# First expert's first weights loaded by GpSimd in rows of 1 KB, and block 1's queries and keys earlier in the order

## The chip, the cores and the metric

The kernel runs on one core of one Trainium2 chip. The metric is the device time of one execution in microseconds (us), the median of several runs. A time line in the text counts from the first instruction of the profiled execution.

## The reference

Two steps follow each other. The first is attention in chunks of 32 queries, each of which sees its own 32 keys, 16 to the left, 8 to the right and 8 memory keys. The second is a mixture of eight experts over the 3072 tokens that come out of it, with weights from a Sinkhorn iteration over all tokens.

```python
# q, k, v: (4, 8, 768, 64); mem_k, mem_v: (4, 8, 8, 64)
for c in range(seq // 32):
    q_c = q[:, :, c*32 : c*32+32]
    k_full = concatenate([mem_k, k[:, :, l_start:r_end]], axis=2)
    v_full = concatenate([mem_v, v[:, :, l_start:r_end]], axis=2)
    scores = scale * matmul(q_c, k_full.transpose(0, 1, 3, 2))
    a = softmax(scores)
    out[:, :, c*32 : c*32+32] = matmul(a, v_full)
x = out.transpose(0, 2, 1, 3).reshape(3072, 512)

# w_gate (512, 8), w1 (8, 512, 1024), w2 (8, 1024, 512)
P = exp(x @ w_gate - max)
for _ in range(8):
    P /= P.sum(1, keepdims=True) + 1e-9
    P /= P.sum(0, keepdims=True) + 1e-9
    P *= 3072 / 8
for e in range(8):
    h = maximum(x @ w1[e], 0)
    out += P[:, e:e+1] * (h @ w2[e])
```

## The kernel before

The tokens are cut into 24 blocks of 128 for the attention and into 6 units of 512 for the experts. TensorE takes a unit through an expert with operands that are split into two half-precision parts (high and low, three products each). Most units use a scheme of seven products for eight (Winograd's form of Strassen's); the first expert's first unit is done plainly, with the matmuls `pp` (first layer) and `yp` (second layer), so that TensorE can begin with weights that are only split and not yet summed.

Weights come in quarters `fp` = 0 to 3 (256 of the 1024 hidden columns each). A quarter of w1 goes through four steps. `load` (line 531) brings it into a stage tile `w1f`. `most` (line 540, tile `mxs`) takes the absolute maximum on VectorE. `scale_w` turns the four maxima into one scale: a reduction `most_of`, a transpose `row_w` and a spread `sp_w` on TensorE, a power of two and its inverse `sw` on VectorE. `plain1` then splits the quarter into its two parts, the high one on ScalarE (line 495), the low one on VectorE (line 503). The operand x of a unit goes the same way: maxima `vmax` over the values `v_pair` (line 956), `row_x`, `sp_x`, `sx`, and a split. For the units after the first, `cut` makes the sums that the seven products need.

The attention of a block n loads q and k (`load_block`), a piece of keys `kx` for the borders, and the values (`load_values`, half by SyncE and half by ScalarE, into `v_pair`, later into tiles that serve as rooms for other things). TensorE transposes them (`tq`, `tk`, `tx`), computes scores `sp`, transposes the weights `ta`, and makes the output `xp` and its transpose `xt`. VectorE takes the maximum `sm`, the difference `s`, the reciprocal `rec` and the scaled output `xq`.

The order on each engine is made ahead of time by a planner, `Plan`. Each piece of work is a task with an engine, a cost and a priority; the planner steps through a modelled time, gives each engine the ready task of lowest priority number, and writes the instructions down in that order. An engine then runs its list strictly in order. For loads the planner keeps a modelled DMA clock, `dma`, which starts at `FIRST`; a load is not issued more than `BEHIND` ahead of it. The numbers `BLOCKS`, `VALUES` and `FIRST` (inside the kernel) are the priorities of the first four blocks' q and k, of their values, and of the first expert's w1 and w2. Where the planner sees TensorE idle for over 0.4 us, `pad` puts `warm` matmuls on the identity there; they are in the list for good and run whether or not the hole is there on the chip.

DMAs of SyncE and ScalarE go by eight counters in turn, and each waits for the earlier one of its counter. Unit 0's operand x is stored as `xkeep` and fetched again for the later experts.

## Time and profile before

| what | before |
|---|---|
| median of 3 runs | 1922.85 us |
| the three runs | 1923.82, 1922.3, 1922.85 us |
| span of the profiled execution, first to last instruction | 1921.2 us |
| median minus that span | 1.65 us |
| TensorE busy | 1905.9 us |
| VectorE busy | 1436.7 us |
| ScalarE busy | 1032.3 us |
| GpSimd busy | 520.3 us |
| packets of DMA, mean rate | 246792, 133 GB/s |

The profiled execution's own device time is not listed apart from the three; the span stands for it, and the median is 1.65 us longer. TensorE is the engine that sets the time: it is busy nearly throughout, and VectorE, ScalarE and GpSimd each have time to spare on average.

### The profile page before, as it was taken

How to read it: one execution, taken by the hardware profiler on the slowest of the kernel's cores; microseconds unless marked ns; L12 is line 12 of the kernel's file. 1: busy time of each engine (PE TensorE's matmuls, PEld its weight loads, DVE VectorE, ACT ScalarE, POOL GpSimd, SP SyncE). 2: the span in 40 equal slices, each digit the busy share in tenths (PEclk: the TensorE clock that was granted, in tenths of full speed). 3: DMA queues.
4: the chain of work that ended last, by engine and by line, in shares of the span. 5: the costliest groups of instructions: out<-in, count | busy, mean ns of one | idle time of the engine just before them, and what ended most of it. 6: DMA issues, size and time to landing. Idle time of an engine off the chain costs nothing.

```text
span 1921.2 us, 47293 instructions
## 1 busy us (share of the span) xinstructions
PE 1905.9 (99%) x19608; PEld 1641.5 (85%) x19608; DVE 1436.7 (75%) x2396; ACT 1032.3 (54%) x2019; POOL 520.3 (27%) x549
## 2 busy tenths in 40 slices
PE   8999999999999999999999999999999999999999
PEld 7676676688888888888888888888888888888888
DVE  5666569778769866897778875898678885786565
ACT  4665564556556545645545554654554564564453
POOL 1220002443224231432124231342124232332112
PEclk9999999999999999999999999999999999999999
DMA  8677653454235342255214533245313632322321
GB/s 197 174 202 205 169 162 122 138 176 144 83 103 173 131 138 94 78 178 186 109 57 148 204 105 127 78 160 171 143 45 99 242 128 92 102 83 83 127 83 67
DMA packets 246792, 254.82 MB, mean 133 GB/s; under 512 B 113265, under 2 KB 180273, under 8 KB 242225
## 3 DMA queue, kind: packets, MB, share of 16 engines
q1 hardware_dynamic: 244452, 251.21, 40.8%
q8 instruction: 153, 2.51, 0.5%
q10 hardware_dynamic: 2124, 0.59, 0.2%
q14 instruction: 63, 0.51, 0.1%
HBM read 187.84 MB, written 63.44 MB: 131 GB/s over the span
## 4 chain that ended last, share of the span: by engine, by line
PE 94%; DVE 3%; issue 1%; DMA 1%; ACT 0%; POOL 0%; SPq 0%; DVEq 0%; POOLq 0%
PE px L1580 26%; PE yx L1580 22%; PE pz L1580 13%; PE yz L1580 11%; PE py L1580 6%; PE yp L2098 6%; PE yy L1580 5%; PE xp L1119 1%; PE sp L1051 1%; PE pp L2017 1%; DVE ss L1738 1%; PE warm L409 1%; PE ta L1109 0%; PE tk L992 0%; PE tq L988 0%
## 5 line engine op out<-in xcount | busy, mean ns | idle before, releaser
L1580 PEld LDWEIGHTS <-w 128*128 128x128 f16 x7896 | 770.9, 98 | 93.1 <-issue 0.8
L1580 PEld LDWEIGHTS <-h 128*128 128x128 f16 x7056 | 689.9, 98 | 82.9 <-issue 2.6
L1580 PE MATMUL px<-x,w 128*128 128x256 f16 x4512 | 549.1, 273 | 0.5 <-issue 0.3
L1903 POOL TENSOR_TENSOR acc<-acc,y 128x256 f32<-128x256 f32 x252 | 265.6, 1060 | 862.4 <-ACT y L1878 839.8
L1580 PE MATMUL yx<-w,h 128*128 128x256 f16 x4032 | 467.6, 273 | 0.7 <-DVE acc L1913 0.6
L1629 ACT ACTIVATE q<-px 128x256 f32<-128x256 f32 x376 | 142.7, 381 | 304.4 <-PE px L1580 299.8
L1580 PE MATMUL pz<-x,w 128*128 128x256 f16 x2256 | 278.4, 273 | 0.0
L1580 PE MATMUL yz<-w,h 128*128 128x256 f16 x2016 | 233.8, 273 | 1.2 <-ACT y L1878 1.2
L1798 DVE TENSOR_TENSOR h<-ss,h 128x1024 f16<-128x1024 f32 x160 | 214.7, 1344 | 3.8 <-ACT h L1774 3.5
L1749 ACT ACTIVATE h<-c 128x768 f16<-128x768 f32 x168 | 140.8, 838 | 109.5 <-DVE c L1639 109.5
L1774 ACT CAST h<-ss 128x1024 f16<-128x1024 f32 x168 | 174.2, 1040 | 24.9 <-DVE ss L1738 24.0
L1738 DVE SCALAR_TENSOR_TENSOR ss<-c,ss 128x256 f32<-128x256 f32 x336 | 172.3, 513 | 8.2
L1782 DVE SCALAR_TENSOR_TENSOR h<-c,h 128x768 f16<-128x768 f32 x168 | 165.0, 982 | 11.2 <-ACT h L1749 11.2
L1639 DVE SCALAR_TENSOR_TENSOR c<-px,q 128x256 f32<-128x256 f32 x188 | 77.7, 421 | 94.2 <-PE px L1580 85.0
L1878 ACT ACTIVATE y<-yx,pscale 128x256 f32<-128x256 f32 x168 | 79.3, 473 | 112.6 <-PE yx L1580 108.8
L1580 PE MATMUL py<-x,w 128*128 128x256 f16 x1128 | 139.2, 273 | 0.0
L1639 DVE SCALAR_TENSOR_TENSOR c<-py,q 128x256 f32<-128x256 f32 x188 | 78.8, 422 | 72.1 <-PE py L1580 66.1
L2098 PE MATMUL yp<-w,h 128*128 128x512 f16 x576 | 131.7, 379 | 0.0
L1738 DVE SCALAR_TENSOR_TENSOR ss<-c,h 128x512 f32<-128x512 f32 x168 | 122.7, 730 | 2.2 <-ACT h L1726 2.2
L1580 PE MATMUL yy<-w,h 128*128 128x256 f16 x1008 | 116.9, 273 | 0.0
L2098 PEld LDWEIGHTS <-h 128*128 128x128 f16 x576 | 55.4, 98 | 58.9
L503 DVE SCALAR_TENSOR_TENSOR w<-ws,sw,w 128x1024 f16<-128x1024 f32 (+1 forms) x64 | 84.9, 1326 | 25.8 <-ACT w L495 25.8
(158 smaller groups left out, 1755.1 us busy)
## 6 DMA issues: line engine op xcount, KB each, us to landing
x<-xkeep SPq DMA_DIRECT2D x28, 1792.0 KB
akeep<-acc SPq DMA_DIRECT2D x168, 256.0 KB
acc<-akeep SPq DMA_DIRECT2D x168, 256.0 KB
w1f<-in_moe_w_dram SPq DMA_DIRECT2D x72, 256.0 KB
w2f<-in_moe_w_dram SPq DMA_DIRECT2D x32, 512.0 KB
w1fm<-in_moe_w_dram SPq DMA_DIRECT2D x56, 256.0 KB
w2fm<-in_moe_w_dram SPq DMA_DIRECT2D x28, 512.0 KB
xkeep<-x SPq DMA_DIRECT2D x6, 1792.0 KB
```

The source lines that it names most:

```text
L503: lambda: nc.vector.scalar_tensor_tensor(dst(1), src(), s, dst(0), op0=ALU.mult, op1=ALU.subtract),
L1580: nc.tensor.matmul(dst.t, a, b, start=(not more and n == 0), stop=(n == end), skip_group_check=more,)
L1629: lambda: nc.scalar.activation(t.t, src.t, AF.Copy, scale=DOWN),
L1639: lambda: nc.vector.scalar_tensor_tensor(c.t[:, o], src.t, DOWN, q.t, op0=ALU.mult, op1=ALU.add),
L1738: lambda: nc.vector.scalar_tensor_tensor(dst(), src(), 0.0, other(), op0=ALU.max, op1=op),
L1749: lambda: nc.scalar.activation(h.t[:, 0, 0:3], c.t, AF.Relu),
L1774: lambda: nc.scalar.copy(h.t[:, 0, 3:7], ss.t),
L1782: lambda: nc.vector.scalar_tensor_tensor(h.t[:, 1, 0:3].rearrange("p a n -> p (a n)"), c.t.rearrange("p a n -> p (a n)"), 0.0, h.t[:, 0, 0 ...
L1798: lambda: spare.tensor_tensor(h.t[:, 1, 3:7], ss.t, h.t[:, 0, 3:7], op=ALU.subtract),
L1878: (lambda: nc.scalar.activation(t.t, src.t, AF.Copy, scale=f))
L1903: lambda: nc.gpsimd.tensor_tensor(acc.t[:, cols], acc.t[:, cols], q.t, op=ALU.add),
L2098: nc.tensor.matmul(py.t, hf.t[:, hl, where[fh], o : o + P], room(fp, WIDE * wl + DM * fh, WIDE * wl + DM * (fh + 1)), start=(fp == 0 and i ...
```

## The change

The planner keeps one DMA clock for SyncE (with ScalarE) and one for GpSimd. The first expert's four w1 quarters are issued by GpSimd, at priority -60 instead of -38; their maxima and the split come at priorities lower by 10 and 8. Every load of a w1 quarter is one DMA of 512 KB with 1 KB in a row instead of two of 256 KB with 512 bytes: a quarter now holds 256 columns that are neighbours, where it held two groups of 128 that lay 512 columns apart. The rows of w2, and the places of the operands (`tile1` for `block1`, `place` in `cut`), follow that order. Block 1's q and k get priority -48 instead of -44.

```diff
--- before.py
+++ after.py
@@ -135,7 +135,7 @@
         clock = {e: 0.0 for e in self.ENGINES}
         waiting = {e: [] for e in self.ENGINES}
         able = {e: [] for e in self.ENGINES}
-        dma = FIRST
+        dma = {"SP": FIRST, "POOL": FIRST}
         for t in self.tasks:
             if t.left == 0:
                 heappush(waiting[t.eng], (t.ready, t.n, t))
@@ -183,11 +183,12 @@
                 t.takes.made = t.takes.make(bank)
             t.start = at
             if t.dma:
-                at = max(at, dma - BEHIND)
+                own = "SP" if t.eng == "ACT" else t.eng
+                at = max(at, dma[own] - BEHIND)
                 t.start = at
                 clock[t.eng] = at + t.cost
-                dma = max(dma, at + t.cost / 2) + t.dma
-                t.end = max(dma, at + t.cost) + 2.6
+                dma[own] = max(dma[own], at + t.cost / 2) + t.dma
+                t.end = max(dma[own], at + t.cost) + 2.6
             else:
                 clock[t.eng] = t.end = at + t.cost
             t.fn()
@@ -510,33 +511,32 @@
         return b
 
 
-    w1v = w1.rearrange("e (kt p) (fh fp f) -> e fp p kt fh f", p=P, fh=2, fp=FP)
-    w2v = w2.rearrange("e (fh fp p) d -> e fp p fh d", fh=2, fp=FP)
+    w1v = w1.rearrange("e (kt p) (fp f) -> e fp p kt f", p=P, fp=FP)
+    w2v = w2.rearrange("e (fp fh p) d -> e fp p fh d", fh=2, fp=FP)
     wo = {}
     known = {}
 
     def load(e, fp, which, prio, ahead="", eng="SP", after=()):
-        shape = [P, 2, KT, P] if which == 1 else [P, 2, DM]
+        shape = [P, KT, 2, P] if which == 1 else [P, 2, DM]
         place = "stage", stage
         if (e, which) == (0, 2) and ahead == "" and fp < 2:
 
             place = ("ws", "ss")[fp], comb
         st = buf(*place, shape, F32, f"w{which}f{ahead}_{e}_{fp}")
 
-        queue = nc.scalar if eng == "ACT" else nc.sync
+        queue = {"ACT": nc.scalar, "POOL": nc.gpsimd, "SP": nc.sync}[eng]
 
         def go():
             if which == 1:
-                for fh in range(2):
-                    queue.dma_start(st.t[:, fh], w1v[e, fp, :, :, fh])
+                queue.dma_start(st.t.rearrange("p k a f -> p k (a f)"), w1v[e, fp])
             else:
                 queue.dma_start(st.t, w2v[e, fp])
 
-        return st, add(eng, 2 if which == 1 else 1, go, after, prio, [st], dma=2.1)
+        return st, add(eng, 1, go, after, prio, [st], dma=2.1 if eng == "SP" else 2.8)
 
     def most(e, fp, which, st, deps, prio):
         def go():
-            flat = st.t.rearrange("p a k f -> p (a k f)" if which == 1 else "p a d -> p (a d)")
+            flat = st.t.rearrange("p k a f -> p (k a f)" if which == 1 else "p a d -> p (a d)")
             nc.vector.tensor_reduce(
                 mxs[:, e, which - 1, fp : fp + 1],
                 flat,
@@ -587,8 +587,8 @@
             return lambda: ws.t[:, i]
 
         if which == 1:
-            a11, a12 = lambda: st.t[:, 0, 0:2], lambda: st.t[:, 0, 2:4]
-            a21, a22 = lambda: st.t[:, 1, 0:2], lambda: st.t[:, 1, 2:4]
+            a11, a12 = lambda: st.t[:, 0:2, 0], lambda: st.t[:, 2:4, 0]
+            a21, a22 = lambda: st.t[:, 0:2, 1], lambda: st.t[:, 2:4, 1]
             ops = [
                 (0, a21, a22, ALU.add),
                 (1, part(0), a11, ALU.subtract),
@@ -618,7 +618,7 @@
             parts = [
                 (
                     lambda j: o.t[:, j, 0:2].rearrange("p o k f -> p (o k) f"),
-                    lambda: st.t[:, 0],
+                    lambda: st.t[:, :, 0],
                     (0.72, 0.85),
                 ),
                 (lambda j: o.t[:, j, 2], a22, (0.5, 0.65)),
@@ -641,13 +641,22 @@
         if e > 0:
             pieces = [(slice(3, 7), slice(0, 4), (1.15, 1.28))]
         else:
-            pieces = [(slice(2, 3), slice(0, 1), (0.5, 0.65)), (slice(4, 7), slice(1, 4), (0.9, 1.1))]
+            pieces = [(None, slice(0, 1), (0.5, 0.65)), (slice(4, 7), slice(1, 4), (0.9, 1.1))]
             deps = deps + o.users
+
+        def place(j, to):
+            if to is None:
+                return o.t.rearrange("p j o k f -> p j (o k) f")[:, j, 1:4:2]
+            return o.t[:, j, to].rearrange(flat)
+
+        def source(to, of):
+            return ws.t[:, 0] if to is None else ws.t[:, of].rearrange(flat)
+
         for to, of, costs in pieces:
             done.append(
                 split(
-                    lambda j, to=to: o.t[:, j, to].rearrange(flat),
-                    lambda of=of: ws.t[:, of].rearrange(flat),
+                    lambda j, to=to: place(j, to),
+                    lambda to=to, of=of: source(to, of),
                     s,
                     deps + sums,
                     prio,
@@ -672,7 +681,7 @@
         o = operands("w1", [P, 2, 7, 2, P], f"w1_0_{fp}")
         done = split(
             lambda j: o.t[:, j, 0:4].rearrange("p o k f -> p (o k f)"),
-            lambda: st.t.rearrange("p a k f -> p (a k f)"),
+            lambda: st.t.rearrange("p k a f -> p (k a f)"),
             sw[:, 0, 0:1],
             [known[0, 1], ld],
             prio,
@@ -682,8 +691,10 @@
         wo[0, fp, 1] = (o, [done])
 
 
-    def block1(e, i):
-        return i if e > 0 else (0, 1, 3, 2, 4, 5, 6)[i]
+    def tile1(e, i, kt):
+        if e > 0 or i > 3:
+            return 2 * i + kt
+        return (0, 4, 5, 1)[i] + 2 * kt
 
     def plain2(fp, st, ld, prio, before):
 
@@ -711,9 +722,9 @@
     lgs = []
     later = []
 
-    BLOCKS = (-50.0, -44.0, -30.0, -26.0)
+    BLOCKS = (-50.0, -48.0, -30.0, -26.0)
     VALUES = (-47.0, -41.0, -28.0, -24.0)
-    FIRST = (-38.0, -20.0)
+    FIRST = (-60.0, -20.0)
 
 
     def needed(n):
@@ -1606,7 +1617,7 @@
             return product(
                 dst,
                 lambda: [
-                    (w.t[:, wl, block1(e, a), kt], x.t[:, xl, b, kt])
+                    (w.t.rearrange("p j o k f -> p j (o k) f")[:, wl, tile1(e, a, kt)], x.t[:, xl, b, kt])
                     for kt in range(2)
                     for wl, xl in PASSES
                 ],
@@ -2016,7 +2027,7 @@
                     ):
                         nc.tensor.matmul(
                             px.t,
-                            w.t[:, wl, 2 * fh + k, kt],
+                            w.t.rearrange("p j o k f -> p j (o k) f")[:, wl, 4 * k + 2 * kt + fh],
                             tokens(k, kt, xl),
                             start=(k == 0 and n == 0),
                             stop=(k == 1 and n == 5),
@@ -2141,15 +2152,17 @@
     def fetch_first(which, at):
         found, staged = [], []
         for fp in range(FP):
-            st, ld = load(0, fp, which, FIRST[which - 1] + 0.5 * fp)
+            st, ld = load(
+                0, fp, which, FIRST[which - 1] + 0.5 * fp, eng="POOL" if which == 1 else "SP"
+            )
             staged.append((st, ld))
             found.append(most(0, fp, which, st, [ld], at - 12.0))
         scale_w(0, which, found, at - 10.0, "att")
         return staged
 
     first2.extend(operands("w2", [P, 2, 7, DH], f"w2_0_{fp}") for fp in range(FP))
-    for fp, s in enumerate(fetch_first(1, START)):
-        plain1(fp, *s, START - 6.0 + 2.0 * fp)
+    for fp, s in enumerate(fetch_first(1, START - 10.0)):
+        plain1(fp, *s, START - 14.0 + 2.0 * fp)
     gate_in[0] = add(
         "SP",
         1,
```

The order of the instructions moves with it. TensorE's list in all has 31995 rows before and 31933 now; 160 and 129 of its matmuls are warm-ups.

SyncE's list near its start, before. `q` and `k` behind the first `kx` row are those of block 1, `v_pair` its half of block 0's values (the rows 16x4x64, 40x4x64 and three of 56x4x64) and then of block 1's:

```order
L772 DMA kx_175<-in_k_dram 32x8x64
L903 DMA v_pair<-in_v_dram 16x4x64
L903 DMA v_pair<-in_v_dram 40x4x64
L903 DMA v_pair<-in_v_dram 56x4x64 x3
L830 DMA q_188<-in_q_dram 128x8x64
L827 DMA k_192<-in_k_dram 128x8x64
L772 DMA kx_175<-in_k_dram 32x8x64 x2
L903 DMA v_pair<-in_v_dram 56x4x64 x4
L531 DMA w1f_0_286<-in_moe_w_dram 128x4x128 x2
L531 DMA w1f_1_334<-in_moe_w_dram 128x4x128 x2
L531 DMA w1f_2_341<-in_moe_w_dram 128x4x128 x2
```

Block 0's values stand directly behind its keys there, and eight w1 rows follow block 1's loads. The same place of SyncE's list now:

```order
L783 DMA kx_179<-in_k_dram 32x8x64
L841 DMA q_183<-in_q_dram 128x8x64
L838 DMA k_191<-in_k_dram 128x8x64
L783 DMA kx_179<-in_k_dram 32x8x64 x2
L914 DMA v_pair<-in_v_dram 16x4x64
L914 DMA v_pair<-in_v_dram 40x4x64
L914 DMA v_pair<-in_v_dram 56x4x64 x7
L841 DMA q_341<-in_q_dram 128x8x64
L838 DMA k_349<-in_k_dram 128x8x64
L533 DMA w2f_0_352<-in_moe_w_dram 128x2x512
L841 DMA q_356<-in_q_dram 128x8x64
```

Block 1's q, k and kx have moved ahead of block 0's values, the eight w1 rows are gone, and the first load of w2 follows the q and k of block 2.

GpSimd's list near its start, before (`ident` is the identity for the warm-ups, the COPY rows fill values into a room):

```order
masks.py:199 ISA
masks.py:199 AFFINE_SELECT ident<-ident 128x128
L303 MEMSET gate 128x128
L920 MEMSET x_room 128x16
L895 COPY w_0_2_360<-v_pair 128x1040
```

No DMA stands there before. The same place of GpSimd's list now:

```order
masks.py:199 AFFINE_SELECT ident<-ident 128x128
L304 MEMSET gate 128x128
L531 DMA w1f_0_163<-in_moe_w_dram 128x4x256
L531 DMA w1f_1_167<-in_moe_w_dram 128x4x256
L531 DMA w1f_2_177<-in_moe_w_dram 128x4x256
L531 DMA w1f_3_185<-in_moe_w_dram 128x4x256
L931 MEMSET x_room 128x16
L906 COPY w_0_2_399<-v_pair 128x1040
```

The four w1 loads stand ahead of everything but the identity and one MEMSET.

VectorE's list near its start, before, from its row 6 on (`mxs` is a maximum of a w1 quarter, `vmax` one of a block's values):

```order
L956 TENSOR_REDUCE vmax<-v_pair 128x1
L1137 TENSOR_SCALAR rec_427<-xp_389 128x8
L1138 RECIPROCAL rec_427<-rec_427 128x8
L1139 TENSOR_TENSOR xq_430<-xp_389,rec_427 128x2x4x64
L956 TENSOR_REDUCE vmax<-v_pair 128x1
L1065 TENSOR_REDUCE sm_480<-sp_434 128x2x4
L1071 TENSOR_TENSOR s_483<-sp_434,sm_480 128x2x4x64
L540 TENSOR_REDUCE mxs<-w1f_0_286 128x1
L540 TENSOR_REDUCE mxs<-w1f_1_334 128x1
L427 TENSOR_REDUCE most_of<-vmax 128x1
L540 TENSOR_REDUCE mxs<-w1f_2_341 128x1
```

The first `vmax` stands at its head there, ahead of all maxima of w1. VectorE's list now, from its row 3 on:

```order
L540 TENSOR_REDUCE mxs<-w1f_0_163 128x1
L540 TENSOR_REDUCE mxs<-w1f_1_167 128x1
L540 TENSOR_REDUCE mxs<-w1f_2_177 128x1
L1073 MEMSET sp_308 32x2x4x16
L1076 TENSOR_REDUCE sm_359<-sp_308 128x2x4
L1082 TENSOR_TENSOR s_373<-sp_308,sm_359 128x2x4x64
L540 TENSOR_REDUCE mxs<-w1f_3_185 128x1
L428 TENSOR_REDUCE most_of<-mxs 128x1
L967 TENSOR_REDUCE vmax<-v_pair 128x1
L1076 TENSOR_REDUCE sm_476<-sp_402 128x2x4
L485 TENSOR_REDUCE most_of<-row_w_0_440 1x1
```

The maxima of w1 have moved from behind the second block's scores to the very front, and the first `vmax` over `v_pair` now stands behind all four of them.

## Rows read from the trace of the kernel before

**Rows 1.** The page: busy time by engine; queue q8 (packets, MB, share).

```profile
PE 1905.9 (99%) x19608; PEld 1641.5 (85%) x19608; DVE 1436.7 (75%) x2396; ACT 1032.3 (54%) x2019; POOL 520.3 (27%) x549
...
q8 instruction: 153, 2.51, 0.5%
```

**Rows 2.** TensorE's waits after 300 us: total us, times, longest.

```profile
PE yz L1580 <- ACT y L1878: 1.2, 1, 1.2
```

**Rows 3.** Timeline of TensorE to 48 us: start, duration, idle before in brackets.

```profile
1.56 7.59 PE L409 MATMUL warm<-ident 128*128 128x256 bf16 x44 [1.56 <-POOL ident masks.py:199]
...
16.68 0.66 PE L1109 MATMUL ta<-ident,s 128*128 128x128 f32 x4 [0.57 <-ACT s L1090]
...
28.92 0.35 PE L463 MATMUL sp_x<-most_of,one 1*128 1x1 f32 x2 [0.22 <-DVE most_of L427]
...
30.56 3.67 PE L409 MATMUL warm<-ident 128*128 128x256 bf16 x32
34.06 1.11 PE L2017 MATMUL pp<-x,w 128*128 128x256 f16 x6
35.10 0.86 PE L1051 MATMUL sp<-kC,qT 64*32 64x64 f32 x64
...
36.56 0.60 PE L988 MATMUL tq<-ident,q 128*128 128x128 f32 x4
36.99 0.60 PE L992 MATMUL tk<-ident,k 128*128 128x128 f32 x4
...
47.18 0.31 PE L1119 MATMUL xp<-w,at 64*32 64x65 f32 x6 [1.83 <-issue]
```

**Rows 4.** TensorE's waits over the span, the two for data behind pp.

```profile
PE xp L1119 <- DVE lg L1412: 1.2, 1, 1.2
...
PE ta L1109 <- DVE most_of L484: 0.4, 1, 0.4
```

**Rows 5.** Timeline of TensorE, 84 to 92 us.

```profile
89.21 1.25 PE L2017 MATMUL pp<-w,w 128*128 128x256 f16 x5 [2.28 <-issue]
```

**Rows 6.** DMA by queue: 35 to 44.4 us, then 79.7 to 86.6 us.

```profile
q1 hardware_dynamic: 3273, 2.62, 97.2%
...
q1 hardware_dynamic: 1718, 2.46, 100.8%
```

**Rows 7.** SyncE's queue in the timeline: start and duration of the issues.

```profile
14.55 5.38 SPq L531 DMA_DIRECT2D w1f<-in_moe_w_dram  x8
...
35.41 0.92 SPq L533 DMA_DIRECT2D w2f<-in_moe_w_dram  x2
...
78.24 0.59 SPq L1238 DMA_DIRECT2D xkeep<-x  x1
```

**Rows 8.** Windows: length, PE PEld DVE ACT POOL busy, clock, DMA share, GB/s.

```profile
2.00:10.00 8.00, 8.00 (x53) 6.32 (x52) 0.00 (x0) 0.87 (x1) 0.00 (x0) 1.00 0.79 155
16.00:24.00 8.00, 6.72 (x172) 5.49 (x171) 6.00 (x9) 4.38 (x10) 1.16 (x2) 1.00 0.96 272
48.00:51.00 3.00, 3.00 (x17) 2.13 (x15) 2.84 (x7) 1.01 (x2) 0.00 (x0) 0.50 0.53 120
```

**Rows 9.** VectorE's instructions by line, 0 to 45 us: total us, mean ns.

```profile
L503 DVE SCALAR_TENSOR_TENSOR w<-w1f,sw,w 128x1024 f16<-128x1024 f32 x4 | 4.9, 1279 | 0.0
L540 DVE TENSOR_REDUCE mxs<-w1f 128x1 f32<-128x1024 f32 x4 | 4.7, 1208 | 0.0
...
L1071 DVE TENSOR_TENSOR s<-sp,sm 128x512 f32<-128x512 f32 x4 | 2.8, 691 | 0.1
...
L503 DVE SCALAR_TENSOR_TENSOR x<-xg,sx,x 128x512 f16<-128x512 f32 x2 | 1.5, 742 | 0.3 <-ACT x L495 0.3
...
L439 DVE RECIPROCAL sx<-ux 128x1 f32<-128x1 f32 x1 | 0.2, 163 | 0.0
```

**Rows 10.** Timeline of VectorE: the last of the four w1 maxima.

```profile
27.03 1.21 DVE L540 TENSOR_REDUCE mxs<-w1f 128x1 f32<-128x1024 f32 x1
```

**Rows 11.** All DMA of the first 24 us.

```profile
DMA packets 13841, 4.56 MB, mean 190 GB/s; under 512 B 9688, under 2 KB 13839, under 8 KB 13839
```

## The prediction

> **What bounds the kernel now.** I read the page first. TensorE is busy for 1905.9 of the 1921.2 us [rows 1], so a gain has to come from one of three things: less work on TensorE, fewer of the 15.3 us in which it stands, or a higher clock. The view of TensorE's waits after 300 us leaves 1.2 us behind ScalarE and less behind VectorE [rows 2]: nothing that the change does for the later experts can be worth a microsecond or two. What is open lies in the first 100 us, which I then read in the timeline.
>
> There TensorE starts at 1.56 us with 44 warm-up matmuls on the identity, then does the attention of the first blocks with warm-ups between, and the first real expert matmul (pp) starts at 34.06 us, behind 32 warm-ups in one piece [rows 3]. Until then it has waited for data six times, between 16.68 and 28.92 us, 1.7 us in all (the bracket at a row's end; first and last of the six shown). So 34.06 - 1.56 - 1.7 = 30.8 us are filled, most with warm-ups: time that is not idle, yet isn't work. Behind the first pp two kinds of wait remain. One is for data, 1.2 us for lg and 0.4 us for a maximum [rows 4]. The other is put down to "issue", 1.83 us at 45.4 us and 2.28 us at 86.9 us [rows 3, 5]; no semaphore ended them.
>
> These two are in the reach of the change, since it moves loads. The page counts 153 packets on the queue of instructions, q8, of 2.51 MB in all, 16.4 KB each, for 2 x 19608 matmuls and weight loads [rows 1], 256 to a packet: TensorE's program arrives in pieces. From 35 to 44.4 us that queue shows no packet at all, while q1 fills 97.2% of the DMA engines with 2.62 MB; from 79.7 to 86.6 us none either, at 100.8% [rows 6]. In front of the first lie the four loads of w2f, 512 KB each, issued from 35.41 us on; in front of the second the store xkeep of 1792 KB, issued at 78.24 us [rows 7]. In both cases the missing packet came when the burst had drained, and TensorE went on then. I read it as a fetch held up by a burst. Behind the first stall the granted clock stood at 0.50, 1.2 GHz, from 48 to 51 us [rows 8], which doubles those 3 us: 1.5 us more. The first stall thus costs 1.83 + 1.5 = 3.3 us, the second 2.28 us, and 3.8 us if the clock answers alike.
>
> **The change part by part.** *Warm-ups.* The order of TensorE's instructions is 31995 rows long before and 31933 now; the 62 are 31 warm-ups, a weight load and a matmul each (160 before, 129 now), because the plan sees smaller holes. The 32 in one piece take 34.06 - 30.56 = 3.50 us, 0.109 us each [rows 3]: 31 are **-3.4 us** of work, 28 of them ahead of the first pp.
>
> *The start.* pp needs the split x of unit 0 and the split w1. In VectorE's order the maxima of w1 now stand first, and the first maximum over v_pair, block 0's values, stands behind all four. From that vmax to the second split of x there lie three maxima over 128x1024 elements (two of v, one of w2f) at 1.21 us, four passes over 128x512 (sm, s, two xq) at 0.69, four splits of w1 at 1.28, two of x at 0.74, and 15 small ones at about 0.16 [rows 9]. That is 3.6 + 2.8 + 5.1 + 1.5 + 2.4 = 15.4 us, if nothing else is late.
>
> When can that vmax start? SyncE's order now puts block 1's q, k and kx ahead of its half of block 0's v, and GpSimd's 2.10 MB of w1 share the engines. By then must have moved: q and k of two blocks (4 x 0.262 MB), kx of two (0.26), three halves of v (0.69), the memory rows (0.13) and w1, 4.23 MB. The DMA engines moved 4.56 MB in the first 24 us at a mean of 190 GB/s [rows 11], by which 4.23 MB take 22.3 us; at the 272 GB/s of 16 to 24 us, when rows of 512 bytes are most of it [rows 8], they take 15.6 us and, from 2 us on, end at 17.6. I take 20, between the two, since half the bytes are w1's longer rows and half the same short ones. So the first pp comes at 20 + 15.4 = 35.4 us (33.0 to 37.7). Work ahead of it: 30.8 - 28 x 0.109 + 1.7 (block 2's sp, 0.8, and its four tq and four tk, 0.43 each from one start to the next, now stand ahead of pp [rows 3]) = 29.4. Waits ahead of it are then 35.4 - 1.56 - 29.4 = 4.4 us where 1.7 were: **+2.7 us** (+0.3 to +5.0).
>
> *Data waits behind pp.* x and w1 are ready in a body when pp starts, and lg's chain starts from the same x. I count half of 1.6 us gone: **-0.8 us** (0 to -1.6).
>
> *The first stall.* w2f_0 and w2f_1 now stand between block 2's and block 3's q and k, ahead of the values of those blocks, and the four loads no longer stand in one piece; the w1 loads have left SyncE. The burst at 35 to 44 us is split, so the fetch finds room: **-3.3 us** (0 to -3.3). *The second stall* stays: the store xkeep is the same 1792 KB, now behind block 4's q, k and kx and not ahead of them, with a fetch due near it: 0 (from -3.8, if the move frees it, to 0).
>
> *Parts at nothing.* SyncE issues 64 DMAs fewer, about 0.5 to 0.7 us each (eight took 5.38 us [rows 7]): 40 us of an engine for which nobody waits after 100 us; if that cover went, a late load would show as a wait for DMA on TensorE, and there is none. The new column order, the strided place in w1's split (128x2x128 instead of 128x256) and tile1 change which 128 columns a matmul reads, not how many. The split could be a little slower on ScalarE and VectorE; VectorE is 75% busy, and 0.1 us on each of 4 would end at the first units' operands, which are ready far ahead.
>
> The sum is -3.4 + 2.7 - 0.8 - 3.3 = -4.8 us against the profiled 1921.2 us span, 1916.4; the median of the three runs is 1.65 us above that span, which gives **1918.0 us**.
>
> **The skill on two of these terms.** The rows show the DMA engines 0.79 busy from 2 to 10 us [rows 8]: a fifth was free for w1. The Trainium skill, page "DMA: Bandwidth & Descriptors", section "Issuing engines are not separate DMA queues", says that DMAs of SP, ACT and GpSimd run on the same 16 engines and interleave; more issuers save issue time alone. By it w1 takes its room from block 0's values, and the vmax starts at the late bound. The same page, section "Queues, rings and completion order", says that each engine goes round robin between queues by packets, so that a lone instruction packet would wait for one packet only. The trace doesn't agree for q8, which got none in 6.9 us at 100.8% of q1; if the rule held here, the first stall would have another cause and could stay.
>
> **The rivals.** (B) *Both stalls go.* For: xkeep moved in SyncE's order; against: it still fills the engines for 7 us with the same bytes, and TensorE runs through 256 instructions in a few us there. Time: 1918.0 - 3.8 = 1914.2.
> (C) *A stall stays or returns.* For: a fetch is due at each 256 instructions, and the attention's short matmuls use up 128 in 0.8 us (64 sp with their loads [rows 3]), so any burst at the wrong place stalls; w1, w2f, v and xkeep are all moved. Against: of the 153 packets [rows 1] only two made TensorE wait. Time: 1918.0 + 3.3 to 3.8, 1921.3 to 1921.8.
> (D) *No room for w1.* The engines are full, block 0's values land at 22.3 us, the first pp comes at 37.7. Time: 1918.0 + 2.3 = 1920.3. For: 0.96 busy from 16 us on [rows 8]. Against: 0.79 before.
> (E) *Slower: GpSimd feeds w1 late.* The trace has no load issued by GpSimd. VectorE works in order and has the fourth w1 maximum ahead of vmax; before, it started at 27.03 us [rows 10]. Now 1.37 us of work lie between its start and vmax, so from 18.6 us on each us that it is late is a us on the first pp, since TensorE has nothing else to do but warm-ups: from 27.3 us on, which is 6.3 us a load from 2 us on, the kernel is slower than 1926.7. SyncE needed 1.35 us for as many bytes (5.38 us for four pairs). At 7 us a load: 30 us, 1918.0 + 11.4 = 1929.4.
>
> **How the numbers follow.** A measurement of this kernel can tell about 0.2% from no change: faster is below 1919.0, slower above 1926.7. The forecast (A) has 0.38: its own range goes from 1915.6 (pp at 33.0) to 1920.3, and 0.32 of it is below 1919.0. B has 0.13, C 0.26, D 0.11, E 0.12. Faster is 0.32 + 0.13 = 0.45; the same 0.06 + 0.26 + 0.11 = 0.43; slower 0.12. The range leaves out E and a little at either end: 1913.8 (B with a margin of 0.4) to 1925.0 (C with the start at its late end: 1921.8 + 2.3, and 0.9 for waits not halved).
>
> **What would show it.** Right: first pp at 33 to 38 us, some 129 warm-ups of 0.109 us in front, w1's fourth maximum over by 18.7 us and vmax over v_pair started at 18 to 22; no wait for "issue" of over 0.5 us between 40 and 60 us, clock 1.00 there, and one such wait behind xkeep; the TensorE rows after 300 us as before. Wrong: a wait for "issue" elsewhere (C); VectorE waiting for w1f's DMA behind 19 us (E) or for v_pair's (D); a new wait of TensorE of over 1 us for data between 36 and 100 us, which I count at nothing.

## The result and the profile after

The changed kernel is slower: 1929.62 us (median of 9 runs, 1923.66 to 1932.09) against 1923.09 us (9 runs, 1922.30 to 1924.69), a ratio of 1.0029 with the interval 1.0021 to 1.0037 (worked out from all the runs; the two medians alone give 1.0034). On a second chip, 12 more runs of it gave 1925.63 us (1921.92 to 1929.69), a ratio of 1.0020 (1.0012 to 1.0029). Not only the middle moved: its runs scatter over 8 us, those of before beside them over 2.4 us. The profiled execution has a span of 1929.6 us and a device time of 1931.35 us, one of its longer runs. In a1, a3 and d4 below one execution took 6346, 7043 and 9179 us; it counts in the median of the table and not in the ratio.

The page of the changed kernel first: busy time by engine, then the queue that is new (packets, MB, share of 16 engines).

```profile
PE 1907.6 (99%) x19577; PEld 1642.4 (85%) x19577; DVE 1439.9 (75%) x2396; ACT 1032.4 (54%) x2019; POOL 522.6 (27%) x553
...
q0 software_dynamic: 576, 2.10, 0.3%
```

TensorE has 31 matmuls fewer than in [rows 1] and yet 1.7 us more busy time: part of it ran at the lower clock (rows below). Queue q0 holds GpSimd's four loads: 2.10 MB in 576 packets, 3.6 KB each.

The waits of TensorE over the whole span (us in total, times, longest):

```profile
PE tq L999 <- DMA q<-in_q_dram: 7.0, 4, 3.7
PE tx L799 <- DMA v_pair<-v_pair: 3.1, 1, 3.1
```

The 7.0 us for q are new, and so is one of 1.67 us behind ScalarE at 90.11 us; against [rows 4] the waits for lg and for the maximum are gone. Where they lie, in TensorE's timeline of the changed kernel (start, duration, idle before):

```profile
15.07 0.66 PE L799 MATMUL tx<-ident,kx 64*128 64x64 f32 x4 [3.07 <-DMA v_pair<-v_pair]
...
18.89 1.19 PE L1062 MATMUL sp<-kC,qT 64*32 64x64 f32 x64 [0.92 <-ACT kC L1020]
...
39.89 2.78 PE L2028 MATMUL pp<-x,w 128*128 128x256 f16 x24
...
107.24 0.63 PE L999 MATMUL tq<-ident,q 128*128 128x128 f32 x4 [1.43 <-DMA q<-in_q_dram]
...
185.55 1.08 PE L999 MATMUL tq<-ident,q 128*128 128x128 f32 x4 [3.73 <-DMA q<-in_q_dram]
```

The start is 39.89 - 34.06 = 5.8 us late [rows 3]. The wait at 15.07 us is put down to v_pair; the transpose there reads kx, and the second profile of the same kernel names kx. Block 0's scores (sp), at 13.40 us before, start at 18.89. No wait for issue is left at 45 us.

The last that block 0's scores waited for is ScalarE and not kx. ScalarE copies the transposed q, k and kx (`qT`, `kC`, `kxT`), and in its list these copies stand behind its own loads of values. Its rows in the changed kernel:

```profile
13.80 1.56 ACTq L901 DMA_DIRECT2D v_pair<-v_pair  x2
...
16.69 0.60 ACT L1027 ACTIVATE qT<-tq 128x512 f32<-128x512 f32 x1
...
17.94 0.41 ACT L806 COPY kxT<-tx 128x256 f32<-128x256 f32 x1
```

And in the kernel before:

```profile
7.53 1.56 ACTq L890 DMA_DIRECT2D v_pair<-v_pair  x2
...
10.42 0.60 ACT L1016 ACTIVATE qT<-tq 128x512 f32<-128x512 f32 x1
```

The issue of v_pair<-v_pair came 6.3 us later, and the copies as much. The transposed kx was ready by 15.73 us, 2.2 us before ScalarE took it up. In c1 below the two come apart: 0.91 us of wait for kx, 2.27 us for ScalarE. Behind the wait for kx the clock was low, as the window from 14 to 24 us shows (length, busy times, clock, DMA share, GB/s):

```profile
14.00:24.00 10.00, 8.01 (x97) 5.85 (x98) 3.57 (x6) 4.98 (x11) 0.66 (x1) 0.50 0.82 121
```

What GpSimd's queue did meanwhile is in the queues' rows from 2 to 14 us, here for the changed kernel and then for the kernel before:

```profile
q0 software_dynamic: 576, 2.10, 51.7%
q1 hardware_dynamic: 2604, 0.65, 24.8%
q10 hardware_dynamic: 1764, 0.42, 18.2%
```

```profile
q1 hardware_dynamic: 5853, 1.45, 60.1%
q10 hardware_dynamic: 2084, 0.58, 26.2%
```

SyncE's queue q1, which brings block 0's and block 1's keys in packets of 250 bytes, moved 0.65 MB for 1.45 MB. More bytes moved in all (3.16 MB for 2.03), but not those that TensorE stood waiting for. SyncE's own rows, of the changed kernel, show it by the last kx of block 0, issued at 9.46 us (6.56 before); block 1's q was issued at 14.18 (10.03 before). Ahead of that kx SyncE waited 3.3 us (1.4 before) for a load of v_pair that ScalarE had issued; the two share their counters.

```profile
9.46 0.32 SPq L783 DMA_DIRECT2D kx<-in_k_dram  x1
...
175.77 0.36 SPq L1249 DMA_DIRECT2D xkeep<-x  x1
176.22 0.40 SPq L841 DMA_DIRECT2D q<-in_q_dram  x1
```

The last two rows belong to the wait of 3.73 us: the q that TensorE waited for was issued right behind the 1792 KB of a store. Before, the same block's q was issued ahead of that store. The window behind the wait shows what else it cost:

```profile
187.00:190.00 3.00, 3.00 (x65) 2.37 (x45) 1.06 (x3) 0.99 (x2) 0.00 (x0) 0.50 0.73 198
```

The granted clock stood at 0.50, 1.2 GHz, from 185 to 190 us. After 400 us the lag of the changed kernel changes by no more than 0.6 us to the end. That lag is the difference of the times at which the same number of matmuls is done, warm-ups not counted; the times at the top are those of the kernel before:

| at (us) | 45 | 50 | 95 | 180 | 190 | 400 | end |
|---|---|---|---|---|---|---|---|
| changed, profiled | +5.1 | +1.6 | -0.8 | +1.6 | +7.7 | +7.4 | +8.0 |
| changed, quick run (a0 below) | +3.7 | +0.2 | -4.2 | -3.2 | -3.4 | -2.0 | -1.4 |

By 95 us the late start was made good in both. In the profiled run 6 of the 8 us were lost at one place, the wait for q at 185 us with the low clock behind it.

### The profile page after: what moved, and what is told of

Same layout as the page of the kernel before. It is cut to its first block, busy times and chain, and to the rows that moved or that the text cites. A ratio compares the mean times of both kernels' runs of the same rounds, so it can differ in the third digit from the quotient of the medians.

```text
span 1929.6 us, 47080 instructions
## 1 busy us (share of the span) xinstructions
PE 1907.6 (99%) x19577; PEld 1642.4 (85%) x19577; DVE 1439.9 (75%) x2396; ACT 1032.4 (54%) x2019; POOL 522.6 (27%) x553
## 4 chain that ended last, share of the span: by engine, by line
PE 94%; DMA 2%; DVE 2%; SPq 1%; issue 1%; POOL 0%; ACT 0%; ACTq 0%; POOLq 0%; DVEq 0%
PE px L1591 25%; PE yx L1591 22%; PE pz L1591 13%; PE yz L1591 11%; PE py L1591 6%; PE yp L2109 6%; PE yy L1591 6%; DMA q<-in_q_dram 1%; PE sp L1062 1%; PE xp L1130 1%; DMA w1f<-in_moe_w_dram 1%; PE tq L999 1%; PE tk L1003 1%; PE xt L1171 0%; PE pp L2028 0%
## 5 line engine op out<-in xcount | busy, mean ns | idle before, releaser
L496 ACT ACTIVATE w<-ws,sw 128x1024 f16<-128x1024 f32 (+1 forms) x64 | 69.5, 1088 | 66.7 <-POOL ws L584 66.7
```

Source lines behind the costliest of these rows:

```text
L496: lambda: nc.scalar.activation(dst(0), src(), AF.Copy, scale=s),
```

## The experiments

Each was timed in five rounds against the kernel before on its chip. "Scores" is the start of block 0's sp, "pp" the first expert matmul, both in the profiled run. Of each edit only the lines that matter are shown; lines without a sign are a summary.

| kernel | median us (runs) | ratio to before, interval | scores, pp (us) |
|---|---|---|---|
| before | 1923.09 (9) | | 13.40, 34.06 |
| changed, second chip (a0) | 1925.63 (12) | 1.0020, 1.0012 to 1.0029 | 18.93, 39.42 |
| store behind q (a1) | 1926.73 (12) | 1.0017, 1.0009 to 1.0026 | 19.89, 40.71 |
| columns alone (a2) | 1922.12 (11) | 0.9996, 0.9987 to 1.0004 | 12.65, 33.31 |
| GpSimd alone (a3) | 1924.77 (11) | 1.0007, 0.9998 to 1.0016 | 18.42, 40.25 |
| before, stores cut (b1) | 1920.92 (11) | 0.9989, 0.9980 to 0.9998 | 12.53, 33.95 |
| changed, stores cut (b2) | 1926.86 (7) | 1.0025, 1.0014 to 1.0036 | 19.02, 39.51 |
| changed, GpSimd held, stores cut (b3) | 1923.15 (11) | 1.0006, 0.9997 to 1.0015 | 12.79, 42.01 |
| plan numbers alone (b4) | 1922.50 (11) | 0.9999, 0.9990 to 1.0008 | 13.10, 33.47 |
| half from GpSimd (c1) | 1923.95 (11) | 1.0004, 0.9995 to 1.0013 | 16.37, 37.68 |
| akeep from ScalarE (c2) | 1942.99 (4) | 1.0104, 1.0090 to 1.0117 | 19.34, 39.98 |
| warm-ups back (c5) | 1926.61 (9) | 1.0021, 1.0011 to 1.0031 | 19.42, 42.65 |
| parts and akeep (c4) | 1938.47 (4) | 1.0081, 1.0068 to 1.0095 | 13.61, 34.26 |
| GpSimd behind block 0 (d1) | 1923.73 (11) | 1.0006, 0.9997 to 1.0015 | 13.30, 38.95 |
| columns, stores cut (d3) | 1920.44 (11) | 0.9988, 0.9979 to 0.9997 | 13.72, 34.37 |
| d1, stores cut (d4) | 1923.94 (11) | 1.0005, 0.9996 to 1.0014 | 12.67, 39.38 |

**The changed kernel again (a0).** No edit.

> The changed kernel once more. In the profile of the changed kernel the start is 5.8 us late (first pp at 39.89 us for 34.06), yet by 157 us it is level with the kernel before, and then TensorE waits 3.73 us for a q at 185.55 us behind the xkeep store of 1792 KB, with the clock at 0.50 behind it. Late-store theory: the runs fall in two groups, near 1924 us (clock 0.998) and near 1930 us (clock 0.995), according to that one wait; a profile near 1924 shows no wait of over 1 us there. Start theory: the loss is the late start, all runs lie above 1926 us apart from noise, and a profile of a quick run shows an earlier first pp.

Its profile was of the quickest run, a span of 1920.1 us. Of its waits (whole span) these are the largest:

```profile
PE tx L799 <- DMA kx<-in_k_dram: 3.3, 1, 3.3
PE sp L1062 <- ACT kC L1020: 2.1, 1, 2.1
```

The late start is the same and no wait for q is there. So the start alone doesn't make the 1929 us: the two profiled runs of this kernel differ by the later waits. The 12 runs form no two groups but a spread from 1921.9 to 1929.7, so one wait that is there or not doesn't make it either.

**One store moved (a1).**

```diff
+            if u == 2:
+                xkept[u].hold = 5
```

(`Plan.run` then issues the store five SyncE tasks later; these lines are not shown.)

> The changed kernel with one DMA moved in SyncE's order: the store xkeep of unit 2 behind the next two blocks' q and k (and one akeep), all else in the order of the changed kernel. Late-store theory: the wait for q near 185 us goes (under 0.5 us), the clock stays at 1.00 from 185 to 190 us, and all runs lie at 1922 to 1925.5 us. Start theory: 1928 to 1931 us as before, the wait was only a place where earlier lateness shows.

The wait for q at 185 us went, as the late-store theory said, but the time didn't: a wait for issue of 1.36 us stood at 185.5 us instead and one of 2.25 us for q at 106.8. That theory falls as the cause of the whole.

**The parts: columns (a2), GpSimd (a3), plan numbers (b4).**

```diff
 a2: the new columns and DMAs, with  add(eng, 2 if which == 1 else 1, ..., dma=2.1), and the old numbers
 a3, on the kernel before:
+        if (e, which, ahead) == (0, 1, ""):
+            queue = nc.gpsimd
 b4, on a2:  BLOCKS -48, fetch_first(1, START - 10.0), plain1 at START - 14.0
```

> The kernel before with the new column order alone: one DMA of 512 KB in rows of 1 KB for each w1 quarter, from SyncE, the strided places, and the plan's numbers as before, so that the order on all engines is that of the kernel before. If the parts that the forecast put at nothing are nothing: 1921.5 to 1924.5 us, first pp within 1 us of 34.06. Rival: the shorter issue and longer rows bring the weights sooner and take room from the attention's loads as GpSimd's do: first pp over 1 us off, time off by over 2 us.

> The kernel before with the first expert's w1 issued from GpSimd (eight DMAs of 256 KB in rows of 512 bytes), order on the compute engines as before. If GpSimd's transfers take the engines from block 0's small rows: w1 lands by 15 us, the last kx of block 0 is issued over 2 us later than 6.56, the first scores (sp) start at 15.5 to 19 us for 13.40, first pp at 36 to 39.5 us for 34.06, time 1924 to 1929 us. Rival: the lateness of the start came from block 1's q and k being ahead of the values; then sp starts within 1 us of 13.40, and the time is 1921 to 1924 us.

> The kernel with the new columns and one DMA for each w1 quarter from SyncE, block 1's q and k at -48, and maxima and split of the first w1 sooner by 10 and 8, but no load from GpSimd, w1's loads at their place of before. If GpSimd's early load is what made the start late: first pp at 33 to 36 us, 1920 to 1924 us. Rival (moving block 1's q and k ahead of the values is the cost): first pp at 37 us or later, 1924 to 1928 us.

The columns cost nothing that shows, nor do block 1's loads and the sooner split. GpSimd's issue alone, in the old order, moves scores and pp by 5.0 and 6.2 us:

```profile
18.42 1.19 PE L1053 MATMUL sp<-kC,qT 64*32 64x64 f32 x64 [2.26 <-ACT kC L1011]
...
40.25 1.11 PE L2019 MATMUL pp<-x,w 128*128 128x256 f16 x6
```

Of these 6.2 us 3.1 came back by 50 us, since the wait for issue at 45 us was gone; the ratio of 1.0007 stands for 1.3 us, not clear of noise. So no part alone shows the loss of the whole change (1.0020 and 1.0029): it came only where GpSimd's early loads and the plan's new order, with 31 warm-ups fewer, stood together. What the two do to each other was not tested apart.

**Half of the bytes (c1), and the same bytes later (d1, d4).**

```diff
 c1, on a3:
+        if (e, which, ahead) == (0, 1, "") and fp < 2:
 d1, on a2, from GpSimd:
+                for _ in range(10):
+                    nc.gpsimd.memset(st.t, 0.0)
```

> The kernel before with half of the first expert's w1 (quarters 0 and 1, 1.05 MB) issued from GpSimd, the other half from SyncE at its old place. With all of it from GpSimd in this order the scores of block 0 started at 18.42 us for 13.40 and pp at 40.25 for 34.06. If the bytes in GpSimd's large packets are what holds up block 0's small rows, half of them cost about half: scores at 15 to 16.5 us, pp at 36 to 38 us, time 1921.5 to 1925 us. Rival (a fixed cost of a GpSimd load or of its queue being in use): scores at 17.5 us or later; or, if the last bytes alone hurt, at 14 us or before.

> The order of before on the compute engines, new columns, and the first expert's w1 from GpSimd, but behind ten memsets of the stage tile (about 10 us, the plan doesn't know of them), when block 0's keys and values are in. If only the collision with block 0 costs: scores at 13.4 us (within 0.7), first pp at 33.5 to 35.5 us, q of blocks 2 to 6 issued 2 us or more sooner than before, 1920 to 1923.5 us. Rival (GpSimd's large packets hold up whatever loads are next, block 1's and 2's here): scores on time, but first pp at 36.5 us or later, 1924 to 1927 us.

> d1 with the xkeep stores cut into four. If leads of q grow with w1 off SyncE and the store's burst is what is left: 1918.5 to 1921 us, faster than both kernels. If neither: 1922 to 1925 us.

Half the bytes cost 3.0 and 3.6 us, six tenths of 5.0 and 6.2. That goes with the early bytes: up to 14 us GpSimd's queue had moved 1.05 MB in c1 and 1.57 MB in a3, whose last two loads went out only at 19.02 us. Issued from 12.02 us on, behind block 0's loads, all of them left the scores alone (13.30 us, with ScalarE's copies from 10.40 us on) and held up what came next: VectorE's second vmax waited 3.47 us for block 1's values (row of d1, VectorE's timeline), and pp came at 38.95.

```profile
24.20 1.22 DVE L971 TENSOR_REDUCE vmax<-v_pair 128x1 f32<-128x1024 f32 x1 [3.47 <-DMA v_pair<-in_v_dram]
```

So it isn't the collision with block 0 in itself: at both places GpSimd's loads held up the small rows beside them. Whether the large packets do it or the early bytes alone isn't shown, since no run sends the same bytes as early from SyncE or in small packets. That SyncE, rid of w1, issued the q of block 2 at 14.9 us for 20.1 brought nothing to the time.

**Cutting the stores (b1, b2, d3), and holding GpSimd in the plan (b3).**

```diff
+            xkept[u] = add("SP", 1, piece(0), done, at + 10.0, [x], dma=7.0)
+            xkept[u].rest = [piece(i) for i in range(1, 4)]
 b3, besides:  seven memsets of w1f as a task of 7.0 us ahead of GpSimd's first load
```

(Each piece has 448 KB; one goes out after each of SyncE's next tasks.)

> The kernel before, with each of the six xkeep stores (1792 KB) cut into four DMAs of 448 KB, each after the next one of SyncE's tasks, all else in the order of before. Burst theory (a store of 1792 KB at a time holds up instruction packets and the loads behind it): the wait for issue at 86.9 us (2.28 us) goes under 0.5 us, the clock stays 1.00 behind it, the stall at 45.4 us stays since w2f is untouched; time 2.3 to 3.8 us less than before, 1918.5 to 1920.5 us. Rival (the bytes in flight matter, not the burst): the stall stays or moves, 1921.5 to 1923.5 us.

> The changed kernel with the six xkeep stores cut the same way. Burst theory: no wait for q of over 1 us near 107 and 185 us, no wait for issue of over 1 us between 80 and 190 us; the late start stays (first pp at 39.5 us or later); runs within 4 us of each other, median 1920 to 1923 us, where the changed kernel had 1925.6 to 1929.6. Rival (the lateness of SyncE's loads comes from the start and from the order of loads, not from the stores): waits stay, median above 1925 us.

> The changed kernel with the stores cut, and GpSimd's first load held up by seven memsets of the stage tile (about 7 us, known to the plan, which orders anew: 155 warm-ups). Start theory (w1's packets of some 3.6 KB take the engines from block 0's packets of 256 bytes): the scores of block 0 start at 13 to 15 us for 18.9, the first pp at 33 to 36.5 us for 39.9; time 1917 to 1921 us. Rival (the order of the loads, block 1 ahead of the values, makes the start late): scores of block 0 on time, but its first values and the first pp still 3 us or more late (37.5 us or more); time 1920 to 1924 us.

> The order of before, new columns from SyncE, xkeep stores cut into four, akeep from SyncE as ever. If the two parts add (0.9996 and 0.9989): 1919.5 to 1921.5 us, a ratio of 0.9980 to 0.9992. If b1 was one program's luck: 1922 to 1924 us.

The burst theory fails: the wait for issue behind the first store stays in b1 (2.83 us at 88.06) and d3 (2.56 us at 86.87), though its pieces went out over 8 and 6 us. From 78 to 86 us q1 was as full as before all the same (95.0% and 105.4% of the engines for 97.7%), so that full engines without one large store remain possible. The changed kernel with cut stores still has waits of 1.22 us for q and 2.31 us for issue. b3 has the scores back at 12.79 us, yet pp at 42.01: the weights, later now (the first maximum of w1 runs at 16.24 us), block 1's kx (2.33 us of wait at 17.98) and the values (vmax waited 2.95 us) hold up the rest. d3 is the fastest kernel of the study, 1920.44 us, faster than both; b1 gives the same. With GpSimd's loads the cut stores are worth nothing that shows (b2 1.0025 beside 1.0020, d4 1.0005 beside d1's 1.0006). Why they are worth some 2 us without them is open. The profiled runs can't tell: b1's is its longest (1922.92 us), d3's is no shorter than a2's (1919.89 and 1919.44). The wait for issue near 47 us is shorter in them (0.73 and 0.52 us, for 1.83 before and 1.9 in a2), but it lies 30 us ahead of the first store.

**What the warm-ups were worth (c5), and akeep off SyncE (c2, c4).**

```diff
 c5:  in fill(b, n), at the piece ahead of the first pp:   n += 31
 c2, c4:  nc.scalar.dma_start(akeep[T], a.t)   for   nc.sync.dma_start(akeep[T], a.t)
```

> The changed kernel with the 31 warm-ups that it lost put back in one piece ahead of its first pp (3.4 us of TensorE's time, nothing else moved): 160 as before. Lead theory: TensorE's start is 3.4 us later and SyncE's isn't, so the loads win lead and the waits for q shrink: the median is at most 1.5 us above that of the changed kernel (1925.6 to 1929.6), or below it. Rival (the loads' lateness follows TensorE's, since their buffers come free when TensorE has read them): all 3.4 us show, 1929 to 1933 us.

> The changed kernel with the twelve akeep stores of the first expert issued from ScalarE, where the sum that they store is made, and not from SyncE, in whose order q and k stand behind them. Lead theory (the late start left SyncE's loads with 3.5 to 6.4 us between a q's issue and its transpose, where the kernel before has 7 us and more, so that TensorE waits wherever a load is held up): the leads of q for blocks 4 to 15 grow by 1 us or more, waits for q of over 1 us go, median 1921 to 1924 us. Rival (SyncE's list isn't what is late, the transfers themselves are): leads and waits as in the changed kernel, median 1925 to 1930 us.

> The order of before on the compute engines with the new column order and one DMA for each w1 quarter from SyncE, the xkeep stores cut into four, and the akeep stores issued from ScalarE; no load from GpSimd. The parts alone gave 0.9996 (columns) and 0.9989 (cut stores). If they add: 1919 to 1921 us, faster than both kernels. Rival (the cut stores were luck of one program): 1921.5 to 1923.5 us.

With 31 warm-ups more, pp starts 2.8 us later (42.65) and the median is the same as without (1926.61, between the changed kernel's 1925.63 and 1929.62; ratio 1.0021 against 1.0020 and 1.0029). The quickest run is not: 1924.93 us, against 1921.92 and 1923.66 for the changed kernel on its two chips. One wait for q is left, 2.6 us. The moved akeep stores didn't test what they were meant to: 20 us (c2) and 16 us (c4) slower than before, and in c2 the leads of q are no longer than in the changed kernel. SyncE's and ScalarE's DMAs take the same eight counters in turn, and in c4 TensorE waited 7.1 us for v_pair; that a store that ScalarE issues late holds up SyncE's loads through a counter was not tested apart.

## Why the prediction was wrong

Two steps failed: the start was mis-sized, and later waits for q, which the sum has at nothing, took the time out of the range.

**The start (+2.7 us)** measured +7.2 by the same sum, beyond its bound of +5.0: from TensorE's start at 1.58 us to the first pp at 39.89 us are 38.3 us, and 29.4 of work leave 8.9 for waits, where 4.4 were forecast and 1.7 were before. Of the 8.9 us TensorE stood for 4.9; the other 4.0 are the 8.0 us that it worked at half clock from 14 to 24 us, counted half (an estimate from that window). The prediction has no term for a low clock here.

In times: pp was forecast for 35.4 us and came 4.5 us later. Of these 3.3 lie in vmax, 23.26 us instead of 20, past the bound of 22.3. The step was "by then must have moved ... 4.23 MB", which priced the loads by their bytes as if all shared one pace, and asked only when vmax's own operands are there. The bytes did move fast, 264 GB/s from 2 to 14 us, but by queue the pace was unequal. And vmax stands in VectorE's order behind block 0's scores, which were 5.5 us late, last of all behind ScalarE. Whether ScalarE's issue of v_pair<-v_pair waited for data or for a shared counter the profile doesn't tell. a3 shows that GpSimd's early loads did it, c1 that the cost grows with the bytes in it, d1 that later loads held up later work. The other 1.2 us lie behind vmax, 16.6 us to pp and not 15.4: VectorE waited 1.66 us at 26.14 us for block 1's scores, which TensorE made late at half clock.

Rival D named the place and asked for bytes; its price, 2.3 us over the forecast, was too small for the same reason. The Trainium skill, page "DMA: Bandwidth & Descriptors", section "Queues, rings and completion order", says that an engine goes round robin between queues by packets. I set that against q8's silence, though no row tells whether a packet of q8 had been asked for by then. For the data queues the rows come near the rule from 8 to 12 us: 339 packets of q0, 267 of q10 and 210 of q1, with 88.1%, 8.4% and 6.4% of the engines' time. From 4 to 8 us they don't: 181, 583 and 825 packets.

**The later waits (at nothing).** With the start's 4.5 us put right, the sum gives 1922.5 us, inside the range and near the quick run's 1921.92. That they meet is in part luck: in the quick run the second stall was shorter too. What lies between the quick run and the profiled one comes later. In the profiled run TensorE waited 7.0 us for q in four places, and the lag grew from 1.6 to 7.7 us around the last of them. The prediction named such a wait among the things that would make it wrong and gave it no price. Why q comes late in some runs and not in others stays open.

**The warm-ups (-3.4 us)** did go, and the median shows nothing of it (c5). The step "31 are -3.4 us of work" took time for TensorE as time for the kernel. A sooner TensorE meets loads that aren't sooner; the quickest runs without them are 1.3 and 3.0 us quicker than the quickest with them, the medians are not. From SyncE's and TensorE's timelines, the issue of q to the start of its transpose, waits included:

| block | before | changed, profiled | changed, quick run | warm-ups back |
|---|---|---|---|---|
| 4 | 36.4 to 43.4: 6.9 | 41.6 to 47.2: 5.6 | 38.9 to 46.0: 7.1 | 39.6 to 49.2: 9.6 |
| 5 | 50.7 to 58.0: 7.3 | 52.6 to 57.0: 4.5 | 50.0 to 54.2: 4.2 | 51.8 to 57.4: 5.6 |
| 9 | 98.2 to 107.7: 9.5 | 102.2 to 107.2: 5.1 | 95.7 to 102.2: 6.5 | 98.9 to 105.9: 7.0 |
| 14 | 151.7 to 166.9: 15.2 | 162.1 to 168.5: 6.4 | 153.3 to 163.7: 10.4 | 159.9 to 166.9: 7.0 |
| 15 | 167.2 to 180.0: 12.8 | 176.2 to 185.6: 9.3 | 167.9 to 176.8: 8.9 | 174.4 to 182.8: 8.4 |

Before, a q has 6.9 us or more here; in the changed kernel 4.2 to 10.4. With less lead, whatever holds up SyncE's list (a store, a late buffer) can end in a wait of TensorE. But the lead alone doesn't tell where: block 5 has 4.2 us in the quick run without a wait, and block 15, the place of the longest wait, has 9.3 us with it and 8.9 in the quick run without. Behind the longest waits stands a stretch at half clock (185 to 190 us above); behind b2's wait for issue of 2.31 us at 85.64 us the clock stayed at 1.00. That the leads make the scatter is an argument from this table, with c5's median for it; that a lead restored brings the time back was not shown, since c2 failed as a test.

**The data waits behind pp (-0.8 us)**: those two went, and the waits for q took their place in the profiled run, not in the quick one.

**The first stall (-3.3 us)** went, as forecast, also in a3, c1 and d1, which kept the old order of the w2f loads; so the reason given, w2f loads in two pieces, isn't what it takes: a later TensorE was enough. That part of the forecast came true without its reason. **The second** stayed, as forecast, in the quick run alone: 1.49 us at 83.3 us, with the clock at 1.00 behind it. In the profiled run no wait for issue of over 0.2 us is left.

**The parts at nothing** in the new columns and the plan's numbers were nothing that shows: a2 0.9996, b4 0.9999. Rival E, GpSimd late with w1, did not come true in its form: the fourth maximum ran at 21.71 us, but behind block 0's late scores, with three of the four done by 13.9 us. The time came out on its side, the slower one, by another mechanism.

## What to carry to other kernels

Before giving a load a queue of its own, ask not whether the engines have room but which small transfers run beside it: beside GpSimd's queue, with packets fourteen times as large, SyncE's moved less than half their bytes (0.65 MB for 1.45), and the work that waited came 5 to 6 us later. Follow that to every engine whose list has loads ahead of work: here the last wait was for ScalarE, though a wait for kx stands ahead of it in TensorE's rows. And before counting saved filler work as time, look at the lead of the loads behind it (issue to first use): where TensorE comes sooner and the loads don't, the saving can turn into waits that come and go from run to run.

## What was not expected of the hardware

GpSimd's loads went out in packets of 3.6 KB for rows of 1 KB, and of 3.3 KB (640 packets for 2.10 MB, a3) for rows of 512 bytes; SyncE's loads of the same weights went in packets under 2 KB (a2, all 1828 packets of q1 from 15 to 20 us). Four GpSimd loads of 512 KB took 3.31 us to issue. A q issued right behind a store of 1792 KB on the same queue was waited for until 9.3 us after its issue (176.22 us to the transpose at 185.55); in the quick run the same q behind the same store was there within 8.9 us, and nothing waited for it.
